# A new order for five engines: the masks of 14 attention tiles leave GpSimd, 38 unread products on TensorE

## The chip, the cores and the metric

The kernel runs on one core of a Trainium2 chip, as one launch. The metric is the device time in microseconds. The core has five engines that run side by side, each through its own list of instructions in order: TensorE (PE; its weight loads are shown as PEld), VectorE (DVE), ScalarE (ACT), GpSimd (POOL), and SyncE (SP), which here issues the transfers. They wait for each other by semaphores.

## The reference

The inputs are q, k, v of 8 batches, 8 heads, 576 positions and 64 columns, s of 8 x 8 x 576, and the weights of a gated unit. First comes a causal attention with a decay that a running sum of s gives, then a causal convolution of five taps, its sigmoid as a gate, and two 512 x 512 products:

```python
scores = scale * np.matmul(q, k.transpose(0, 1, 3, 2))
cum = np.cumsum(np.maximum(s, 0.0), axis=-1)
bias = -(cum[:, :, :, None] - cum[:, :, None, :])
scores = np.where(causal, -1000000000.0, scores + np.minimum(bias, 0.0))
attn = np.exp(scores - np.max(scores, axis=-1, keepdims=True))
attn = attn / (np.sum(attn, axis=-1, keepdims=True) + 1e-09)
x = np.matmul(attn, v)                 # heads side by side: (8, 576, 512)
for k in range(5):
    gate_pre += conv_w[k][None, None, :] * xp[:, k:k + S, :]   # xp: x with 4 zero rows ahead
gate = 1.0 / (1.0 + np.exp(-gate_pre))
out = gate * (x @ w_val) @ w_out
```

## The kernel before, in words

The work is cut into 32 tiles n = 4b + p: batch b, pair of heads p. ORDER is one long text of steps written as `name.index:engine:slots`, where S is SP, T TensorE, A ACT, V DVE and G POOL. Each engine gets its steps in the order of the text; how the steps of two engines stand to each other in the text does not matter. The slots name PSUM banks (0 to 7) or numbered buffers in SBUF. What is computed is the same for every order; the order, the choice of engine and the buffers decide who waits for whom.

The steps of one tile are these.

- `ld_q`, `ld_k`, `ld_t`, `ld_v`, `ld_s`, `ld_cw`, `ld_wv`, `ld_wo`: transfers into SBUF. V of a batch comes in five pieces (`ld_v.b.0` to `ld_v.b.4`, L471; for batch 0 by pairs of heads, L467 and L468), into one of two buffers `vst`.
- `c_q`, `c_k`, `cast_wv`, `cast_wo`: casts to bf16 (L373, a helper that copies on whatever engine it is given).
- `qt`, `qq`, `tt`: transposes of q and k on TensorE (L489, L629, L480), `qe` and `te` copy them out of PSUM (L373).
- `vp`: V times the decay weight `w`, for one pair of heads, on POOL (L474).
- `s0`, `s1`, `s2`: the scores of the tile in three steps (L505), each followed by an exponential `e0`, `e1`, `e2` on ACT into a buffer of P (L556). There are three buffers of P. `s4` and `e4` do the last 64 rows.
- The causal mask of the diagonal blocks is done in one of two ways. Where a step `mk.n` (or `ml.n`) stands in ORDER, POOL zeroes the upper part of P behind the exponential (L579). Where none stands, TensorE adds a large negative number in PSUM ahead of the exponential, with one further product for each of the two heads (`future`, L518).
- `av0`, `av`: P times V' (L594) into a pair of banks; `rec` and `nm` divide by the sums (L607, L613); `xt` transposes the result (L626), `xe` copies it to `xT` (L373).
- The convolution: `t1` on DVE (L665), then the taps `t2`, `t3`, `t4`. Each of these is either one step on DVE (L670), or a product `p2`, `p3`, `p4` on POOL (L654) or ACT (L652) and a sum on POOL (L673).
- `th`: the gate as a tanh on ACT (L690, L684); `val`: the product with `w_val` (L703); `glu`: gate times value on DVE (L712).
- `out` for each 128 rows of two batches (L723), `oe` copies the result out of PSUM (L373), `st` stores it (L731).
- `wu`: a product whose result nobody reads (L620).

Tiles 28 to 31, the last batch, are cut in two parts of 384 and 192 positions: scores `u0` to `u3`, exponentials `f0` to `f3` (L570), and `av.n.h`, `xt.n.h` and so on. At the end a check of the sums (`chk`, `cnt`, `cntc`, `flag`) decides whether a slow general path must run; with these inputs it does not.

In the list before, the P buffer of a tile was named by its score step, as the second slot of `s0.n` (`s0.0:T:0+1:0`), and kept for the whole tile.

Of the kernel before, what the change touches and what calls it, by code (L numbers as in the profile page):

```python
# [16 lines left out]
B, H, S, D = 8, 8, 576, 64  # L17
# [179 lines left out]
s2.0:T:6+7 wu.15:T:0 c_q.0.2:G e1.0:A qt.0.1.q:T:3 wu.16:T:0 qe.0.1.q:V wu.17:T:0 wu.18:T:0 e4.0.0:A wu.19:T:0  # L197
centre:V s0.1:T:4+5:1 ld_k.1.0:S:2 s2.1:T:2+3 e0.1:A qt.0.2.q:T:1 c_k.0.2:V decT:T:0 ld_cw:S e2.0:A qt.0.2.k:T:4
mk.1:G wu.20:T:5 ld_k.1.1:S qe.0.2.k:V wu.21:T:5 wu.22:T:5 qe.0.2.q:A s1.1:T:6+7 c_k.0.3:V e2.1:A s0.2:T:4+5:2
c_q.0.3:G ld_v.0.2:S expw:A qt.0.3.q:T:1 e1.1:A s4.0.1:T:2+3 qe.0.3.q:V vp.0.0:G qt.0.3.k:T:0 qe.0.3.k:V e4.0.1:A  # L200
ld_q.1.0:S:3 e0.2:A s2.2:T:6+7 s1.2:T:2+3 vp.0.1:G av0.0:T:0+1 e2.2:A av.0:T ld_v.0.3:S mk.2:G rec.0:V av0.1:T:4+5
e1.2:A nm.0:V av.1:T c_k.1.0:G:2 s0.3:T:6+7:0 rec.1:V s2.3:T:2+3 e0.3:A nm.1:V ld_t.1:S cwT:T:0 xt.0:T:1 c_k.1.1:G
cwc:V xt.1:T:4 e2.3:A wu.23:T:6 xe.0:V ld_q.1.1:S vp.0.2:G qq.1.1:T:0:7 t1.0:V:0 s4.0.2:T:2+3 s1.3:T:5+6 e4.0.2:A
xe.1:V c_q.1.0:A:0 s4.0.3:T:2+3 mk.3:G t3.0:V ld_v.1.2:S e4.0.3:A t1.1:V:1 e1.3:A ld_v.1.1:S av0.2:T:2+3 vp.0.3:G
av.2:T t2.0:V ld_v.1.0:S qe.1.3:A tt.1:T:5 ld_v.1.3:S qe.1.2:V p4.1:G:0 p4.0:A:1 ld_v.1.4:S ld_wv:S:4 av0.3:T:6+7
av.3:T te.1:A rec.2:V ld_t.2:S t4.1:G c_q.1.1:G nm.2:V s0.6:T:0+1:1 rec.3:V xt.2:T:5 nm.3:V e0.6:A t4.0:G s0.7:T:2+3:2
# [5 lines left out]
s1.7:T:6+7 nm.6:V e2.5:A xt.4:T:0 ld_v.2.2:S c_q.2:G:1 tt.2:T:1 xe.4:V th.0:A:2 av0.5:T:2+3 t1.4:V:2 av.5:T te.2:A  # L212
ld_v.2.4:S val.3.0:T:4 th.3:A:3 p4.4:G:1 rec.5:V val.3.1:T:1 nm.5:V e1.7:A val.1.0:T:5 glu.3.0:V t4.4:G xt.5:T:2
c_k.2:A:2 glu.3.1:V ld_v.2.1:S val.1.1:T:3 glu.1.0:V s2.7:T:6+7 glu.1.1:V qq.2.0:T:1:5 vp.1.3:G xe.5:V val.0.0:T:3
t2.4:V e2.7:A val.0.1:T:4 t1.5:V:1 p2.5:G:0 qe.2.0:A av0.7:T:6+7 glu.0.0:V glu.0.1:V ld_v.2.3:S val.2.0:T:3 t2.5:G
p3.5:A:1 t3.4:V av.7:T ld_v.2.0:S qe.2.1:A qq.2.1:T:4:2 ld_k.5:S:4 rec.7:V cast_wo:G nm.7:V val.2.1:T:0 qe.2.3:A
xt.6:T:5 glu.2.0:V xt.7:T:1 xe.6:V qe.2.2:A s0.9:T:6+7:1 glu.2.1:V s1.9:T:2+3 p4.5:G:0 xe.7:V out.0.2:T:0 e0.9:A
# [15 lines left out]
glu.8.1:V oe.0.5:A:5 ld_k.6:S:0 glu.10.1:V val.9.1:T:1 mk.14:G t4.11:V th.9:A:4 s2.14:T:2+3 qq.5.0:T:7:6 e2.14:A
glu.9.0:V c_k.5:G:0 av0.13:T:4+5 qe.5.0:V av.13:T qe.5.1:A val.11.0:T:0 ld_v.4.4:S rec.13:V glu.9.1:V th.11:A:1
s1.14:T:2+3 s0.15:T:6+7:0 nm.13:V vp.3.2:G e1.14:A val.11.1:T:1 glu.11.0:V xt.13:T:4 ld_v.4.0:S glu.11.1:V e0.15:A
mk.12:G s1.15:T:2+3 xe.13:V s2.15:T:0+1 st.0.5:S t1.13:V:2 e2.15:A qq.5.1:T:7:6 c_q.4:G:1 out.1.1:T:5 t2.13:V qe.5.2:A
qe.5.3:V av0.14:T:0+1 e1.15:A c_k.4:G:2 av.14:T out.1.2:T:7 rec.14:V p4.13:A:0 nm.14:V oe.1.1:A:2 qq.4.0:T:6:2
# [10 lines left out]
av0.18:T:1+2 ld_t.7:S e0.19:A av.18:T glu.15.1:V c_q.6:G:1 rec.18:V s1.19:T:6+7 glu.15.0:V s2.19:T:3+4 e1.19:A nm.18:V
out.1.4:T:0 t2.16:V e2.19:A xt.18:T:1 ld_v.6.0:S vp.5.3:G s0.20:T:6+7:1 xe.18:V tt.6:T:5 e0.20:A oe.1.4:V:1
qq.6.1:T:4:3 mk.19:G t1.18:V:2 th.16:A:1 st.1.3:S av0.17:T:6+7 te.6:V av.17:T qe.6.3:A c_q.7:G:2 ld_v.6.3:S  # L250
qq.6.0:T:0:2 rec.17:V qe.6.2:A nm.17:V out.1.6:T:5 t3.18:V qe.6.0:A ld_v.6.4:S av0.19:T:6+7 p2.18:G:1 oe.1.6:V:5
# [45 lines left out]
def main_path(ctx, tc, q, k, v, s, moe_w_val, moe_conv_w, moe_w_out, out, okcnt):  # L297
# [44 lines left out]
    Ps = kind("P", [128, 2, 1536], BF16)  # L342
# [315 lines left out]
    def tap(m):  # L658
# [181 lines left out]
```

## Time and profile before

| | before |
|---|---|
| median of 3 runs | 188.22 us |
| runs | 188.03, 190.68, 188.22 us |
| span of the profiled execution | 187.6 us |
| median less span | 0.6 us |
| mean granted clock of TensorE | 0.999 |
| instructions | 6637 |
| bytes read, written | 30.57 MB, 9.44 MB |

The page gives of the profiled execution its span alone, from the first to the last instruction; what lies around it is taken as the 0.6 us by which the median of the runs is longer.

The page lists for each engine its busy time and share of the span, then the span in 40 slices, the transfers by queue, the chain of work that ended last with each engine's share, and the costliest groups of instructions. A row of such a group ends with the busy time of all of them, the mean duration of one in ns, and, behind the second bar, the idle time of the engine just before them with what ended it. Busy times are unions: instructions of one engine that overlap are counted once, so a count times the mean is a little more than the busy time.

### The profile page before, as it was taken

To read this page: it belongs to the slowest core of one execution; us is meant where nothing else is said; L and a number is where in the kernel's file an instruction comes from. 1 tells how busy PE (TensorE), PEld (TensorE's weight loads), DVE (VectorE), ACT (ScalarE), POOL (GpSimd) and SP (SyncE) were. 2 spreads that over 40 slices of the span, in tenths; PEclk is the share of its full clock that TensorE was granted. 3 is DMA by queue.
4 is the path that set the end of the run, shared out by engine and by line. 5 is a ranking of instruction groups with operands and counts; after the bars stand their busy time and mean duration, and the time that the engine had idled before them with its cause. 6 is when DMAs were issued, how large, how long until landed. Compare 5 with 4: busy or idle time off the path is not lost.

```text
span 187.6 us, 6637 instructions
## 1 busy us (share of the span) xinstructions
PE 170.1 (91%) x2704; PEld 113.5 (60%) x2720; DVE 163.3 (87%) x321; ACT 170.6 (91%) x230; POOL 164.5 (88%) x149
## 2 busy tenths in 40 slices
PE   6898885888899998998978999999999999999991
PEld 2556573476757765576745667586566865776560
DVE  4355999878997899999999899998989899999980
ACT  2589899899999999999999999999999999999772
POOL 5267999899999999999978999999999989899610
PEclk9999999999999999999999999999999999999999
DMA  5998999999999999999298999899541003401164
GB/s 164 274 277 246 231 225 243 343 388 341 193 232 304 277 303 258 389 270 283 71 248 184 274 333 325 193 314 247 164 162 66 3 0 115 171 3 56 61 224 175
DMA packets 62283, 40.46 MB, mean 216 GB/s; under 512 B 47333, under 2 KB 49381, under 8 KB 62250
## 3 DMA queue, kind: packets, MB, share of 16 engines
q1 hardware_dynamic: 61706, 39.49, 77.1%
q8 instruction: 22, 0.36, 0.8%
q10 hardware_dynamic: 544, 0.52, 0.8%
q14 instruction: 11, 0.09, 0.2%
HBM read 30.57 MB, written 9.44 MB: 213 GB/s over the span
## 4 chain that ended last, share of the span: by engine, by line
PE 50%; ACT 15%; SPq 9%; DMA 8%; issue 6%; POOL 5%; DVE 4%; ACTq 0%; POOLq 0%; DVEq 0%
PE bank L723 14%; PE bank L703 11%; PE bank L594 10%; ACT P L556 9%; PE bank L505 7%; DMA vst<-in_v_dram 6%; SPq L435 3%; PE bank L629 3%; PE bank L626 3%; POOL gp L673 2%; DMA first<-in_k_dram 2%; ACT th L690 2%; SPq L471 2%; ACT QKT L373 2%; SPq L467 2%
## 5 line engine op out<-in xcount | busy, mean ns | idle before, releaser
L556 ACT ACTIVATE P<-bank 128x1024 bf16<-128x1024 f32 x84 | 82.9, 1042 | 4.1 <-PE bank L505 3.0
L670 DVE SCALAR_TENSOR_TENSOR gp<-bank,cwr,gp 128x574 f32<-128x574 bf16 (+6 forms) x72 | 52.3, 740 | 0.9 <-POOL gp L673 0.5
L673 POOL TENSOR_TENSOR gp<-gp,pr 128x572 f32<-128x572 f32 (+6 forms) x36 | 45.1, 1259 | 4.4 <-DVE gp L670 1.7
L474 POOL TENSOR_TENSOR Vp<-vst,w 128x650 bf16<-128x650 f32 x32 | 40.7, 1288 | 2.8 <-DMA vst<-in_v_dram 1.8
L505 PE MATMUL bank<-QKT 64*128 64x128 bf16 (+4 forms) x592 | 37.2, 237 | 4.8 <-ACT P L556 1.8
L703 PE MATMUL bank<-xT,wv 128*128 128x288 bf16 (+2 forms) x256 | 38.5, 287 | 1.1 <-ACT P L556 0.5
L594 PE MATMUL bank<-Vp,P 128*128 128x65 bf16 x960 | 36.0, 194 | 2.4 <-POOL Vp L474 1.1
L594 PEld LDWEIGHTS <-P 128*128 128x128 bf16 x960 | 33.2, 97 | 6.8 <-issue 1.5
L723 PE MATMUL bank<-wo,glu 128*128 128x512 bf16 x128 | 34.1, 380 | 1.5 <-issue 0.5
L505 PEld LDWEIGHTS <-QKT 64*128 64x128 bf16 x592 | 19.4, 94 | 22.3 <-issue 14.6
L712 DVE SCALAR_TENSOR_TENSOR glu<-th,bank 128x288 bf16<-128x288 f32 (+2 forms) x64 | 27.5, 445 | 2.0 <-ACT th L690 0.9
L703 PEld LDWEIGHTS <-wv 128*128 128x128 bf16 x256 | 22.4, 97 | 11.0 <-issue 4.8
L654 POOL TENSOR_TENSOR pr<-xT,cwr 128x572 f32<-128x572 bf16 (+6 forms) x28 | 28.3, 1020 | 0.6 <-ACT xT L373 0.6
L373 ACT COPY QKT<-bank 128x1024 bf16<-128x1024 bf16 (+1 forms) x26 | 24.2, 966 | 3.8 <-PE bank L489 2.9
L613 DVE TENSOR_TENSOR xn<-bank,recs 128x640 bf16<-128x640 f32 (+2 forms) x36 | 26.8, 745 | 0.6
L665 DVE SCALAR_TENSOR_TENSOR gp<-xT,cwr,bank 128x576 f32<-128x576 bf16 (+2 forms) x36 | 26.4, 741 | 0.7
L579 POOL TENSOR_SCALAR_AFFINE_SELECT P<-P 128x1024 bf16<-128x1024 bf16 (+1 forms) x22 | 22.3, 1021 | 4.2 <-ACT P L556 4.2
L690 ACT ACTIVATE th<-gp,cwr 128x576 f32<-128x576 f32 x28 | 22.0, 794 | 0.1
L723 PEld LDWEIGHTS <-glu 128*128 128x128 bf16 x144 | 12.4, 98 | 13.2 <-issue 1.6
L373 ACT COPY ot<-bank 128x512 f32<-128x512 f32 x26 | 15.2, 610 | 1.5 <-PE bank L723 1.0
L626 PE MATMUL bank<-ident,xn 128*128 128x128 bf16 x164 | 14.9, 219 | 0.7 <-ACT P L556 0.3
L373 POOL CAST qkb<-qkf 128x2048 bf16<-128x2048 f32 (+1 forms) x9 | 14.4, 1619 | 0.0
(66 smaller groups left out, 174.8 us busy)
## 6 DMA issues: line engine op xcount, KB each, us to landing
out_dram<-ot SPq DMA_DIRECT2D x36, 256.0 KB, 4.3
vst<-in_v_dram SPq DMA_DIRECT2D x28, 256.0 KB, 5.9
first<-in_q_dram SPq DMA_DIRECT2D x6, 512.0 KB, 6.0
first<-in_k_dram SPq DMA_DIRECT2D x6, 512.0 KB, 6.2
qkf<-in_q_dram SPq DMA_DIRECT2D x6, 512.0 KB, 6.7
qkf<-in_k_dram SPq DMA_DIRECT2D x6, 512.0 KB, 7.3
vst<-in_v_dram SPq DMA_DIRECT2D x15, 128.0 KB, 5.4
first<-in_q_dram SPq DMA_DIRECT2D x4, 256.0 KB, 5.3
```

Source lines behind the costliest of these rows:

```text
L373: (act.copy if e is act else e.tensor_copy)(dst, src)
L474: e.tensor_tensor(Vps[b % 2][:, :, HP[p]], vslot(b)[:, :, HP[p]], w[:, :, b * 8 + 2 * p:b * 8 + 2 * p + 2].unsqueeze(3).to_broadcast([128, ...
L505: pe.matmul(ps[:, hh, c0:c0 + nq], QKTs[b % 2][r, 1, p, k0:k0 + 128], QKTs[b % 2][r, 0, p, q0:q0 + nq], **kw)
L556: act.activation(out=Pt(n)[:, :, step * 512:(step + 1) * 512], in_=pair((f"s{step}", n)), func=AF.Exp, scale=0.125)
L594: pe.matmul(ps[:, o:o + 65], lhsT, Vps[b % 2][:, kb, 2 * p + w, :], start=(kb == 0), stop=(kb == qb))
L613: vec.tensor_tensor(xns[b % 2][:, g, p * 128:(p + 1) * 128].rearrange("t g (w d) -> t w g d", w=2), ps[:, :, :, 0:64], recs[:, n, :, g].un ...
L654: pool.tensor_tensor(pr, xTs[b % 2][:, c, 4 + lo - m:4 + hi - m], r.to_broadcast([128, hi - lo]), ALU.mult)
L670: vec.scalar_tensor_tensor(gp[:, lo:hi], xps(n, *h)[:, lo - m:hi - m], r, gp[:, lo:hi], ALU.mult, ALU.add)
L673: pool.tensor_tensor(gp[:, lo:hi], gp[:, lo:hi], prs[at[f"p{m}", n, *h][0]][:, lo:hi], ALU.add)
L703: pe.matmul(ps, wv[:, dc, c * 128:(c + 1) * 128], xTs[b % 2][:, dc, 4 + lo:4 + hi], start=(dc == 0), stop=(dc == 3))
L712: vec.scalar_tensor_tensor(glu2[:, c, o + lo:o + hi], th[:, lo:hi], 1.0, ps, ALU.add, ALU.mult)
L723: pe.matmul(bank_of(u, i), glu2[:, c, i * 128:i * 128 + 128], wo[:, c, :], start=(c == 0), stop=(c == 3))
```

## The change

ORDER is written anew. SP's 110 steps are the same in the same order, and ACT issues the same two first loads of k. On the other engines these things differ.

- Masks: `mk` stands for 5 tiles (11, 14, 19, 22, 23) instead of 18 (0 to 4, 6, 7, 9, 11 to 14, 18 to 20, 22, 24, 27), and `ml` for none instead of 4. All other tiles are masked by products on TensorE.
- Unread products: 38 instead of 32. Twelve stand ahead of the first transposes instead of eight.
- Choices of engine, by count of steps:

| steps | before | after |
|---|---|---|
| `qe` on ACT, DVE | 26, 10 | 27, 9 |
| `oe` on ACT, DVE | 26, 10 | 29, 7 |
| `xe` on ACT, DVE | 12, 24 | 9, 27 |
| `c_q`, `c_k` on ACT, DVE, POOL | 3, 4, 17 | 2, 2, 20 |
| `p2`, `p3`, `p4` on ACT, POOL | 8, 28 | 6, 31 |
| `t2`, `t3`, `t4` on DVE, POOL | 72, 36 | 71, 37 |

- The order of the steps on all engines but SP, the PSUM banks, and the buffers of P, `th`, `ot`, `pr`, `gp`, `qkb`. The slot of P now stands at the exponentials (`e0.0:A:0`), each of which names it.
- In the code, `Pt` looks the buffer up there, `split` is a set made ahead, and `val_part` loses a case that is not used.

The diff, cut: of ORDER the beginning, the stretch up to `av.4`, and the end.

```diff
 ORDER = """
-ld_k.0.0:A ld_q.0.0:S ld_k.0.1:A wu.0:T:0 ld_t.0:S wu.1:T:7 wu.2:T:0 wu.3:T:7 ld_s:S wu.4:T:0 ld_q.0.1:S wu.5:T:7
-wu.6:T:0 ld_q.0.2:S wu.7:T:7 c_k.0.0:V ld_k.0.2:S qt.0.0.k:T:0 wu.8:T:2 c_q.0.0:V ld_v.0.1:S qe.0.0.k:A qt.0.0.q:T:1
-wu.9:T:7 c_k.0.1:G qe.0.0.q:A wu.10:T:2 wu.11:T:7 s0.0:T:0+1:0 e0.0:A tt.0:T:2 ld_q.0.3:S relu:V qt.0.1.k:T:3
-wu.12:T:4 ld_k.0.3:S te.0:A wu.13:T:7 scan:V mk.0:G wu.14:T:0 ld_v.0.0:S qe.0.1.k:A s1.0:T:1+2 s4.0.0:T:4+5 c_q.0.1:A
...
-xe.2:V s2.6:T:6+7 e0.7:A qq.1.0:T:0:1 t1.2:V:2 mk.6:G p2.1:A:0 s1.6:T:2+3 t3.2:V qe.1.0:A ld_q.2:S:0 mk.7:G qe.1.1:V
-e2.6:A t3.1:V s1.4:T:0+1 e1.6:A s0.4:T:6+7:0 t2.2:V ld_k.2:S:1 xt.3:T:4 e0.4:A s0.5:T:2+3:0 t2.1:G t4.2:V s2.4:T:6+7
-xe.3:V wu.24:T:5 e2.4:A vp.1.0:G mk.4:G wu.25:T:5 t1.3:V:3 wu.26:T:5 wu.27:T:5 ld_wo:S:2 wu.28:T:5 e1.4:A s4.1.3:T:6+7
-ld_t.3:S t3.3:V wu.29:T:5 wu.30:T:5 e4.1.3:A s1.5:T:0+1 t4.3:V wu.31:T:5 th.2:A:0 ld_q.3:S:3 vp.1.2:G av0.4:T:6+7
-th.1:A:1 av.4:T t2.3:V e0.5:A vp.1.1:G cast_wv:G rec.4:V av0.6:T:4+5 nm.4:V av.6:T e1.5:A s2.5:T:2+3 rec.6:V
...
-u2.31:T:4+5:2 f3.30:A nm.28.1:V av.29.1:T:0 t1.31.0:V:1 ml.30:G val.28.0:T:1 f2.31:A t4.30.0:G rec.29.1:V t3.31.0:V
...
-st.3.1:S val.29.0:T:0 th.30.0:A:1 p4.28.1:G:0 t1.28.1:V:0 th.29.0:A:0 t2.31.0:V u3.31:T:5+6 t2.28.1:G out.3.3:T:1
-f3.31:A rec.30.1:V glu.29.0:V t4.28.1:G nm.30.1:V th.31.0:A:4 xt.29.1:T:7 ml.31:G val.31.0:T:0 glu.30.0:V xe.29.1:A
-t3.28.1:V xt.30.1:T:4 p3.29.1:G:1 av.31.1:T:3 glu.31.0:V xe.30.1:A th.28.1:A:2 out.3.0:T:2 t1.30.1:V:3 t1.29.1:V:2
...
+ld_q.0.0:S ld_k.0.0:A ld_k.0.1:A ld_t.0:S ld_s:S ld_q.0.1:S ld_q.0.2:S ld_k.0.2:S ld_v.0.1:S c_k.0.0:G c_q.0.0:A
+c_k.0.1:V wu.0:T:7 wu.1:T:6 wu.2:T:7 wu.3:T:6 wu.4:T:7 wu.5:T:6 wu.6:T:7 wu.7:T:6 wu.8:T:7 wu.9:T:6 wu.10:T:7
+wu.11:T:6 qt.0.0.q:T:0 qt.0.0.k:T:1 qe.0.0.q:A qt.0.1.k:T:2 qe.0.0.k:V ld_q.0.3:S qe.0.1.k:A wu.12:T:7 wu.13:T:6
+wu.14:T:7 s0.0:T:3+4 ld_k.0.3:S tt.0:T:5 e0.0:A:0 ld_v.0.0:S relu:V c_q.0.1:G scan:V te.0:A wu.15:T:2 wu.16:T:1
...
+wu.36:T:7 s4.1.3:T:6+7 s1.4:T:2+3 t3.3:V e4.1.3:A s0.4:T:4+5 e1.4:A:2 s1.5:T:6+7 ld_q.2:S:0 t4.3:V e1.5:A:1 s2.4:T:2+3
+t2.3:V ld_k.2:S:1 e2.4:A:2 t1.2:V:3 s2.5:T:6+7 vp.1.0:G t3.2:V e0.4:A:2 s0.5:T:2+3 ld_wo:S:2 t4.2:V vp.1.2:G e2.5:A:1
+wu.37:T:0 av0.4:T:4+5 av.4:T:4+5 t2.2:V ld_t.3:S e0.5:A:1 vp.1.1:G av.6:T:6+7 rec.4:V nm.4:V av0.6:T:6+7 th.3:A:1
+cast_wv:G th.2:A:2 rec.6:V av0.5:T:0+1 nm.6:V av.5:T:0+1 th.1:A:3 xt.4:T:2 rec.5:V s0.7:T:4+5 nm.5:V ld_q.3:S:3 xe.4:A
+s1.7:T:6+7 e0.7:A:2 val.0.1:T:3 t1.4:V:0 val.3.1:T:0 e1.7:A:2 c_q.2:G:1 t3.4:V val.1.1:T:1 val.3.0:T:4 glu.0.1:V
...
+av.28.1:T:1 f3.31:A:2 rec.29.1:V nm.29.1:V u2.31:T:4+5 t4.29.0:G rec.28.1:V th.31.0:A:0 xt.29.1:T:7 nm.28.1:V
+val.31.0:T:0 xe.29.1:V f2.31:A:2 t1.29.1:V:2 p2.29.1:G:0 xt.28.1:T:2 av.30.1:T:3 t4.29.1:V th.29.0:A:1 glu.31.0:V
+av.31.1:T:1 t2.29.1:G p3.29.1:A:1 xe.28.1:V out.3.0:T:4 t1.28.1:V:3 t3.29.1:G rec.31.1:V rec.30.1:V p4.28.1:G:0
...
 """
...
-    Pt = lambda n, h=None: Ps[at["s0" if h is None else f"u{2 * h}", n][1]]
+    split = lambda n: n in splits
+
+    def Pt(n, h=None):
+        steps = ("e0", "e1", "e2") if h is None else (f"f{2 * h}", f"f{2 * h + 1}")
+        return Ps[next(at[f, n] for f in steps if (f, n) in at)[0]]
...
     def val_part(n, hf):
-        two = at["val", n, 0][0]
-        j = two[hf] if isinstance(two, list) else at["val", n, hf][0]
+        j = at["val", n, hf][0]
...
+    splits = {int(name.split(".")[1]) for name, *_ in steps if name.startswith("u0.")}
```

More of the change, by code (lines that the diff above doesn't have):

```diff
@@ L198 @@
[L198 to L202, printed above, removed]
@@ L213 @@
[L213 to L217, printed above, removed]
@@ L233 @@
[L233 to L237, printed above, removed]
@@ L248 @@
[L248 to L251, printed above, removed]
-s2.20:T:3+4 xt.17:T:0 e2.20:A t4.18:V mk.20:G av.19:T ld_v.6.2:S out.1.5:T:5 xe.17:V qe.6.1:A rec.19:V t2.18:G
@@ new lines @@
+t3.11:V ld_v.4.2:S e0.13:A:0 val.10.1:T:1 ld_v.4.1:S t2.11:V vp.3.1:G val.9.0:T:2 e2.13:A:0 val.8.0:T:6 t4.11:V
+val.9.1:T:7 th.9:A:1 glu.10.1:V val.10.0:T:3 glu.8.0:V th.11:A:2 c_q.4:G:0 st.0.4:S val.11.0:T:4 glu.9.0:V glu.10.0:V
+s1.13:T:5+6 qq.5.0:T:1:2 glu.9.1:V e1.13:A:0 glu.11.0:V val.11.1:T:3 qe.5.0:V vp.3.0:G qe.5.1:A s2.14:T:4+5
+qq.4.0:T:7:6 glu.11.1:V e2.14:A:2 vp.3.3:G av.13:T:1+2 ld_k.6:S:0 glu.8.1:V qe.4.0:V av0.13:T:1+2 qe.4.1:A s1.15:T:4+5
+mk.14:G out.0.5:T:3 ld_v.4.4:S rec.13:V e1.15:A:0 nm.13:V c_k.4:G:1 s1.14:T:6+7 oe.0.5:A:0 ld_v.4.0:S xt.13:T:0
```

162 lines of the change are left out of this document (89 added, 73 removed).

## The prediction

> **What bounds the kernel now.** I read the page first: the busy shares, the clock, the shares of the chain that ended last. Then busy time by stage, then the chain and the waits at the two ends.
>
> ```profile
> span 187.6 us, 6637 instructions
> PE 170.1 (91%) x2704; PEld 113.5 (60%) x2720; DVE 163.3 (87%) x321; ACT 170.6 (91%) x230; POOL 164.5 (88%) x149
> PEclk9999999999999999999999999999999999999999
> PE 50%; ACT 15%; SPq 9%; DMA 8%; issue 6%; POOL 5%; DVE 4%; ACTq 0%; POOLq 0%; DVEq 0%
> 0.00:40.00 40.00, 32.59 (x502) 20.36 (x503) 29.31 (x57) 32.03 (x43) 30.68 (x37) 1.00 0.99 259
> 40.00:130.00 90.00, 84.87 (x1476) 58.70 (x1484) 83.44 (x150) 87.42 (x109) 88.10 (x67) 1.00 1.02 270
> 130.00:150.00 20.00, 19.41 (x332) 13.09 (x333) 18.74 (x34) 19.97 (x26) 19.61 (x17) 1.00 0.31 100
> 150.00:180.00 30.00, 29.74 (x383) 19.62 (x385) 29.49 (x73) 28.24 (x50) 26.10 (x31) 1.00 0.19 69
> 180.00:188.00 8.00, 3.49 (x22) 1.71 (x20) 2.31 (x11) 2.97 (x7) 0.00 (x0) 0.96 0.58 212
> ```
>
> The stage rows give, after the length, the busy time of PE, PEld, DVE, ACT, POOL, then clock, DMA share and GB/s. From 40 to 180 us ACT is busy 87.42 + 19.97 + 28.24 = 135.63 of 140: it idles 4.4 us in all. POOL is busy 88.10 of 90 between 40 and 130. No engine is loafing, so time can only go where load on ACT and POOL goes, and from the ends.
>
> TensorE looks as full (84.87 of 90), but its rows overlap:
>
> ```profile
> L518 PE MATMUL bank<-fut,fut 64*128 64x512 bf16 x20 | 3.8, 376 | 0.0
> 53.46 0.22 PE bank L518 x2
> 176.72 1.73 PE bank L723 x8
> 1.44 3.60 PE L620 MATMUL bank<-ident 128*128 128x512 bf16 x8 [1.44 <-POOL ident masks.py:199]
> ```
>
> Two mask products, each listed at 376 ns, took 0.22 us together on the chain; eight 512-column output products took 1.73 us, 0.216 each. So about half of a listed duration is pipeline, and PE has room that its 91% hides. I take 0.216 us for each pair of mask products (the two heads run side by side) and for each unread product once the array is fast. The Trainium skill says the same of this row: "Perfetto Trace Analysis", Identifying the Most-Contended Engine, calls matmul busy time a bad measure and points to weight-load busy, here 60%. By the listed durations the masks would cost 26 x 0.376 = 9.8 us, by the chain 2.8; the chain is measured, and the other reading is the slow rival below.
>
> **The front** is set by transfers:
>
> ```profile
> 28.08 5.99 DMA vst<-in_v_dram
> 34.23 1.28 POOL Vp L474
> 36.61 1.11 PE bank L594 x30
> 33.69 1.94 ACT L556 ACTIVATE P<-bank 128x1024 bf16<-128x1024 f32 x2 [0.54 <-PE bank L505]
> 37.77 2.85 ACT L556 ACTIVATE P<-bank 128x1024 bf16<-128x1024 f32 x3 [0.33 <-PE bank L594]
> PE bank L505 <- DVE QKT L373: 1.8, 1, 1.8
> PEld L594 <- POOL P L579: 0.7, 2, 0.5
> ```
>
> V of batch 1 lands at 34.1, is scaled (vp.1.0), and only then can av.4 run and free a buffer of P. SP's 110 steps stand in the same order in both lists, so this landing does not move by itself. ACT loses 0.54 and 0.33 us around this gate.
>
> **The change, part by part.** I counted the steps of both lists by engine; a half tile counts as 2/3 (384 columns) or 1/3 (192).
>
> ```profile
> L579 POOL TENSOR_SCALAR_AFFINE_SELECT P<-P 128x1024 bf16<-128x1024 bf16 x18 | 20.6, 1153 | 4.2 <-ACT P L556 4.2
> L579 POOL TENSOR_SCALAR_AFFINE_SELECT P<-P 128x256 bf16<-128x256 bf16 x4 | 1.7, 426 | 0.0
> L556 ACT ACTIVATE P<-bank 128x1024 bf16<-128x1024 f32 x84 | 82.9, 1042 | 4.1 <-PE bank L505 3.0 <-issue 0.4 <-PE bank L594 0.3
> L373 ACT COPY QKT<-bank 128x1024 bf16<-128x1024 bf16 x22 | 21.8, 1034 | 0.7 <-PE bank L629 0.6
> L373 ACT COPY ot<-bank 128x512 f32<-128x512 f32 x26 | 15.2, 610 | 1.5 <-PE bank L723 1.0 <-ACT ot L373 0.6
> L373 ACT COPY xT<-bank 128x576 bf16<-128x576 bf16 x7 | 4.6, 656 | 0.0
> L652 ACT ACTIVATE pr<-bank,cwr 128x572 f32<-128x572 bf16 x4 | 3.2, 789 | 0.0
> L373 ACT CAST qkb<-first 128x2048 bf16<-128x2048 f32 x1 | 1.9, 1898 | 0.0
> L373 ACT CAST qkb<-first 128x512 bf16<-128x512 f32 x1 | 0.6, 641 | 0.0
> L373 POOL CAST qkb<-first 128x512 bf16<-128x512 f32 x3 | 1.8, 610 | 2.2 <-DMA first<-in_k_dram 2.2
> L654 POOL TENSOR_TENSOR pr<-xT,cwr 128x572 f32<-128x572 bf16 x9 | 10.3, 1147 | 0.2 <-ACT xT L373 0.2
> L673 POOL TENSOR_TENSOR gp<-gp,pr 128x572 f32<-128x572 f32 x13 | 18.3, 1406 | 1.7 <-DVE gp L670 1.3
> L670 DVE SCALAR_TENSOR_TENSOR gp<-bank,cwr,gp 128x572 f32<-128x572 bf16 x15 | 12.0, 803 | 0.1
> L373 DVE COPY ot<-bank 128x512 f32<-128x512 f32 x10 | 6.8, 683 | 0.0
> L373 DVE COPY QKT<-bank 128x1024 bf16<-128x1024 bf16 x6 | 7.3, 1217 | 0.0
> ```
>
> *ACT.* QKT copies: four come from DVE, three go; net two whole less a half: 2 x 1.034 - 0.52 = +1.55. Output copies +3: 3 x 0.610 = +1.83. xT copies: net one whole less, -0.66. Casts: c_k.2 (1.898) and c_q.1.0 (half of it, 0.95) leave; net one of 512 columns comes, +0.64: -2.2. Tap products: 7.33 whole ones become 4.33: -3 x 0.789 = -2.37. Sum **-1.9 us**.
>
> *POOL.* Masks 18 to 5: -13 x 1.153 = -15.0; the four small ones, -1.7. Casts +1.9 + 0.95 + 0.61 = +3.5. Tap products +1.67 x 1.147 = +1.9; tap sums -1.33 x 1.406 = -1.9. Sum **-13.2 us**.
>
> *DVE.* -3 x 0.683, -2 x 1.217 + 0.6 for copies out, +0.45 for xT (a guess from its size, bounded by 0 and ACT's 0.66), two casts of about 0.6 less, taps +1.33 x 0.803: **-3.5 us**.
>
> *PE.* Masks by product: 13 x 0.216 = +2.8, the four small ones under 0.2 each. Six more unread products: +1.3. Fourteen masks leave POOL and one, 23, comes. Seven of the fourteen, n = 0 to 4, 6 and 7, lie in the front, where PE is busy 32.59 of 40 even by its long rows: ACT's work hides them. Without that cover they cost 0.22 each. The other seven lie where PE has room by the start-to-start times.
>
> *The first steps.* Twelve unread products instead of eight stand ahead of the first transposes. Here one takes 3.60 / 8 = 0.45, so the transposes start about 1.1 us later (12 x 0.43 from 1.44) and the first exponential about 0.5, since three casts now run side by side. The gate at 34 us hides it; uncovered it is 0.5 to 1.8. Queued behind these products is all of PE.
>
> *The gate.* Ahead of the exponential that waits for av.4's buffer (e0.7 in the new list, e0.5 in the old) ACT has 21 exponentials instead of 19, 2 x 1.042, and with its smaller steps about 2.9 us more by the listed durations. So the idle 0.54 + 0.33 = 0.9 should go: -0.9, between 0 and -2.9. What is late next is ACT itself.
>
> *The masks' path.* Exponential, mask on POOL, product becomes exponential, product. The waits for masks are small (the 0.7 above), but POOL holds 5% of the chain, 9.4 us; its load falls by 13.2 / 164.5 = 8%, so I take -0.7, between 0 and -4.4 (all of ACT's idle from 40 to 180).
>
> *The tail.*
>
> ```profile
> 173.94 0.27 PE bank L505 x4
> 176.00 0.17 PE bank L626 x3
> 176.17 0.55 PE bank L594 x18
> 183.47 0.59 ACT ot L373
> ```
>
> After the last score product PE works without pause to the last copy. There the new list has one more attention half (0.55) and one more group of transposes (0.17): **+0.7**, between 0 and +1.4. ACT's work behind its last exponential is as long as before.
>
> *Banks, buffers, stores.* Moved PSUM banks change no work; the wait they could add lies between -0.5 and +1.8 (the longest PE wait above). I take 0, nearest to the many waits under 0.5. Stores sit in SP's list ahead of later loads as before, so a late output copy could hold a load; the copies stand no later relative to their neighbours, so 0. The other edits rename tests (`split`, `Pt`) and emit nothing.
>
> Sum on the profiled execution: 187.6 - 1.9 - 0.9 - 0.7 + 0.7 = 184.8. The median of the runs, 188.22, is 0.6 above this span; so **185.4 us**.
>
> **The rivals.**
>
> *POOL set the pace.* For: 88.10 of 90. Against: few waits name it. Then the masks' path brings 2.2 to 4.4 instead of 0.7: 183.9 to 181.7, middle **182.8**.
>
> *Nothing comes of it.* ACT's 1.9 reappears as waits, since every tile still passes through all four engines, and 0.9 + 0.7 stay too: **188.2**. That is also where it ends if the new list doesn't do what it says, that is if ACT's busy time stays at 170.6. For: ACT holds only 15% of the chain. Against: its 4.4 us of idle.
>
> *TensorE becomes the bound* (slower). For: half the chain is PE. If the listed 376 ns were real, 26 of them are 9.8 us; half of that, PE's share of the chain, is 4.9: 187.6 + 4.9 + 0.6 = **193**. It decides once PE's true load fills a stage, which from 150 on (29.74 of 30, start-to-start in an unbroken row) is nearest. Against: of the masks only 24, 27 and the small ones lie there.
>
> *The clock falls.* At the start a product takes 0.45 instead of 0.216; a spell of 3.6 us like that one loses 1.8: **187.2**. Against: 1.00 in every stage, though PE once waited 1.8 us. The Trainium skill, "TensorE: Matmul & The Clock Gate", Part 1, has the array halve its rate after an idle window of about 3.4 us; no wait here is so long, and the trace's slow start agrees.
>
> **How the numbers follow.** Two per cent, 3.8 us, is about what a measurement of this kernel can tell from no change: faster is below 184.5, slower above 192.0. Forecast (184.5 to 187) 0.37; POOL 0.37; nothing 0.13; clock 0.03; TensorE 0.10. So faster 0.37, same 0.53, slower 0.10. The range leaves out the slow rival and a little below: 181.5 to 190.5. The forecast's own is 184.5 to 187.
>
> **What would show it.** Right: ACT's busy time near 168.7, POOL's near 151, DVE's near 160; the mask line on POOL 5 times, the mask products on PE (L518) 84 times instead of 50; vp.1.0 again near 34.2; ACT without idle at 37; clock 1.00. Wrong: vp.1.0 later than 35 (a transfer moved after all); waits of ACT for L505 above 5 us (masks slow the scores); ACT idle above 6 us from 40 to 180; a clock below 1.00.

## The result and the profile after

| | before | after |
|---|---|---|
| median of 20 runs each | 188.80 us | 189.88 us |
| ratio after / before, 95% interval | | 1.0057 [1.0038, 1.0076] |
| median span | 187.1 us (27 runs of the first set of experiments) | 188.0 us |
| median of time less span | 1.7 us (the same runs: 1.67 to 1.86) | 1.9 us |
| profiled execution: span, time | 187.6 us, not known | 187.3 us, 189.09 us |

In the experiments below, executions more than 1.5% above the fastest of their kernel are left out of ratios and medians.

The new order is 1.1 us slower where the forecast had it 2.8 us faster. ScalarE's load moved about as counted, GpSimd's by less. The first fence is the page of the new order: busy shares, clock, shares of the chain that ended last.

```profile
span 187.3 us, 6728 instructions
PE 174.0 (93%) x2742; PEld 114.7 (61%) x2760; DVE 165.2 (88%) x317; ACT 168.5 (90%) x228; POOL 154.4 (82%) x139
PEclk9999999999999999999999999999999999999999
PE 26%; DVE 25%; POOL 15%; ACT 9%; issue 9%; DMA 2%; SPq 0%; ACTq 0%; DVEq 0%; POOLq 0%
```

ACT is at 168.5 (168.7 was forecast), POOL at 154.4, 10 us below before (13 were forecast), and still the time doesn't follow. The chain of this execution has another make-up: TensorE held half of it, now it holds a quarter, and DVE and POOL hold 40%. The stages (length; busy PE, PEld, DVE, ACT, POOL; clock, DMA share, GB/s) tell where the room went:

```profile
0.00:40.00 40.00, 34.60 (x552) 21.38 (x552) 29.39 (x58) 31.87 (x43) 25.84 (x33) 1.00 0.99 266
40.00:130.00 90.00, 86.83 (x1464) 59.00 (x1473) 84.63 (x147) 87.46 (x112) 81.59 (x60) 1.00 1.03 274
130.00:150.00 20.00, 19.72 (x337) 13.65 (x338) 19.43 (x37) 20.00 (x27) 19.69 (x17) 1.00 0.18 67
150.00:180.00 30.00, 29.66 (x384) 19.16 (x386) 28.81 (x65) 26.55 (x46) 26.46 (x31) 1.00 0.20 72
180.00:188.00 8.00, 3.20 (x21) 1.47 (x18) 2.92 (x14) 2.60 (x6) 0.86 (x2) 0.94 0.54 201
```

POOL's relief lies wholly before 130 us (25.84 against 30.68, 81.59 against 88.10); from 130 on it has as much as before. ACT's relief is not in the full stage from 40 to 130 at all (87.46 against 87.42) but from 150 to 180 (26.55 against 28.24), where it waits. From 40 to 180 us ACT now idles 6.0 us instead of 4.4. The waits of the new order say on what (engine, line, what it waited for: us, times, longest):

```profile
POOL pr L659 <- ACT xT L375: 5.7, 3, 3.4
POOL pr L659 <- DVE xT L375: 5.5, 2, 3.4
ACT th L687 <- POOL gp L678: 1.9, 3, 0.9
```

POOL's list is in order: freed of the masks it stands before the next tap product and waits for a copy of `xT`, 11 us in five waits. In the tail ACT now waits for POOL's tap sums, a wait that before did not have. The end of the chain (start, us, what):

```profile
176.75 0.60 POOL gp L678
177.42 0.60 POOL gp L678
178.09 0.60 POOL gp L678
...
180.97 0.46 ACT th L687
181.46 0.36 DVE glu L714
181.87 1.27 PE bank L725 x5
183.21 0.59 ACT ot L375
```

Before, TensorE worked without pause up to the last copy; now, in this execution, TensorE's last products wait for gate and tap sums. How little that wait is worth, a_tail shows below.

### The profile page after: what moved, and what is told of

Read it like the earlier page. It is cut to its first block, busy times and chain, and to the rows that moved or that the text cites. A ratio compares the mean times of both kernels' runs of the same rounds, so it can differ in the third digit from the quotient of the medians.

```text
span 187.3 us, 6728 instructions
## 1 busy us (share of the span) xinstructions
PE 174.0 (93%) x2742; PEld 114.7 (61%) x2760; DVE 165.2 (88%) x317; ACT 168.5 (90%) x228; POOL 154.4 (82%) x139
## 4 chain that ended last, share of the span: by engine, by line
PE 26%; DVE 25%; POOL 15%; ACT 9%; issue 9%; DMA 2%; SPq 0%; ACTq 0%; DVEq 0%; POOLq 0%
DVE gp L675 8%; PE bank L705 6%; DVE gp L670 5%; PE bank L725 5%; POOL Vp L476 5%; PE bank L599 5%; PE bank L507 5%; POOL gp L678 5%; DVE xn L618 5%; ACT P L562 4%; POOL pr L659 4%; DVE glu L714 4%; DVE xT L375 2%; DMA out_dram<-ot 2%; ACT ot L375 2%
## 5 line engine op out<-in xcount | busy, mean ns | idle before, releaser
L675 DVE SCALAR_TENSOR_TENSOR gp<-bank,cwr,gp 128x573 f32<-128x573 bf16 (+5 forms) x71 | 54.5, 769 | 2.0
L678 POOL TENSOR_TENSOR gp<-gp,pr 128x572 f32<-128x572 f32 (+6 forms) x37 | 43.7, 1182 | 3.2 <-ACT pr L657 0.7
L659 POOL TENSOR_TENSOR pr<-xT,cwr 128x572 f32<-128x572 bf16 (+6 forms) x31 | 30.4, 987 | 11.8 <-ACT xT L375 5.7
L705 PE MATMUL bank<-xT,wv 128*128 128x288 bf16 (+2 forms) x256 | 36.9, 287 | 0.7 <-ACT P L562 0.7
L599 PEld LDWEIGHTS <-P 128*128 128x128 bf16 x960 | 32.1, 98 | 4.7 <-ACT P L562 1.2
L599 PE MATMUL bank<-Vp,P 128*128 128x65 bf16 x960 | 34.1, 194 | 0.7 <-ACT P L562 0.5
L714 DVE SCALAR_TENSOR_TENSOR glu<-th,bank 128x288 bf16<-128x288 f32 (+2 forms) x64 | 26.0, 448 | 1.6 <-ACT th L693 0.5
L375 ACT COPY QKT<-bank 128x1024 bf16<-128x1024 bf16 (+1 forms) x27 | 25.6, 990 | 1.9 <-PE bank L491 1.9
L375 POOL CAST qkb<-first 128x2048 bf16<-128x2048 f32 (+1 forms) x10 | 15.0, 1506 | 6.4 <-DMA first<-in_k_dram 3.3
L375 ACT COPY ot<-bank 128x512 f32<-128x512 f32 x29 | 17.2, 609 | 1.2 <-PE bank L725 1.2
(65 smaller groups left out, 168.5 us busy)
```

The costliest lines, as they stand in the source:

```text
L375: (act.copy if e is act else e.tensor_copy)(dst, src)
L599: pe.matmul(ps[:, o:o + 65], lhsT, Vps[b % 2][:, kb, 2 * p + w, :], start=(kb == 0), stop=(kb == qb))
L659: pool.tensor_tensor(pr, xTs[b % 2][:, c, 4 + lo - m:4 + hi - m], r.to_broadcast([128, hi - lo]), ALU.mult)
L675: vec.scalar_tensor_tensor(gp[:, lo:hi], xps(n, *h)[:, lo - m:hi - m], r, gp[:, lo:hi], ALU.mult, ALU.add)
L678: pool.tensor_tensor(gp[:, lo:hi], gp[:, lo:hi], prs[at[f"p{m}", n, *h][0]][:, lo:hi], ALU.add)
L705: pe.matmul(ps, wv[:, dc, c * 128:(c + 1) * 128], xTs[b % 2][:, dc, 4 + lo:4 + hi], start=(dc == 0), stop=(dc == 3))
```

## The experiments

All ratios are against the old order run beside them. "Span" is the median span of a kernel's runs. The new order stands at 1.0057.

**1. What lies around the span.** In the profiled execution of the new order 1.8 us lay outside the span, where the forecast had taken 0.6 for the old. Its trace shows a last fetch of 8192 bytes of instructions at 189.0 us, behind the span's end, which the old one's does not, and its VectorE program has 518 instructions, the old one's 512. So: the old order once more, the new one with 511, the old one with 520.

> The old order once more, so that each of its runs has a span beside its time. In the profiled executions the new order's time is 1.8 to 1.9 us longer than its span (189.09 against 187.3), the old one's 0.5 (188.03 against 187.6). Theory one (a step outside the span): every run here shows 0.4 to 0.6, and the median span is about 188.3, equal to or above the new order's 187.9. Rival (the 0.5 is the profiler's accident, the loss lies inside the span): the difference scatters, and is about 1.8 here too.

```diff
-        e.memset(vst[:, :, :, 64:65], 2.0)
+        pool.memset(vst[:, :, :, 64:65], 2.0)
... (and three more fills at the start)
```

> The new order with seven small fills at the start given to GpSimd, so that VectorE's program has 511 instructions instead of 518 (the old order's has 512); all that is computed stays. Theory one (the new order's time outside the span is VectorE's end that lies beyond the 512th instruction, for which 8192 more bytes are fetched at 189.0): time less span falls from 1.85 to 0.5, the span stays near 187.9, the median is 188.5, ratio 0.998 to the old order. Rival (the time outside has another cause): time less span stays 1.8, median 189.9, ratio 1.006.

```diff
     vec.memset(onec, 1.0)
+    spare = one.tile([128, 8], BF16, name="spare")
+    for j in range(8):
+        vec.memset(spare[:, j:j + 1], 0.0)
```

> The old order with eight fills of one column of a spare tile added at VectorE's start: 520 instructions instead of 512, about 0.5 us of work under the first transfers. Theory one (program length beyond 512): the span stays, time less span rises from 0.5 to 1.8, the median from 188.8 to 190.1, ratio 1.007. Rival (no step): ratio 1.000, time less span 0.5.

| | ratio, 95% | median | span | time less span |
|---|---|---|---|---|
| before_again | 1.0002 [0.9961, 1.0043] | 188.63 | 186.9 | 1.71 |
| a_dve_less | 1.0037 [1.0007, 1.0068] | 189.75 | 187.8 | 1.86 |
| b_dve_more | 0.9997 [0.9965, 1.0030] | 188.68 | 187.0 | 1.74 |

The program's length is worth nothing, and the theory falls. The late fetch does not follow that length either: a_dve_less, with 511 instructions, still has it (at 189.4), and b_dve_more, with 520, has none. The old order's own runs have 1.7 us outside the span. So the 0.6 of the forecast was no property of the kernel: it was the median of some runs less the span of another, longer execution, whose own time was probably near 187.6 + 1.7 = 189.3.

**2. The masks.** The 14 whole tiles and four small parts that changed sides, in four ways: by products in the old order; nowhere in the old order; nowhere in the new order; five of them back on POOL in the new order.

```diff
 b_masks_pe: mk.n of 14 tiles and ml.28 to ml.31 are taken out of ORDER
 b_no_masks, a_no_masks: besides, no product in their place
+    on_pool |= {("mk", n) for n in (0, 1, 2, 3, 4, 6, 7, 9, 12, 13, 18, 20, 24, 27)} | {("ml", n) for n in (28, 29, 30, 31)}
 a_masks_5: mk.9, mk.12, mk.13, mk.18, mk.20 on POOL, each behind its tile's last exponential
```

> The old order with nothing moved but the masks: the 14 of whole tiles that the new order also does by products, and the four small ones, leave GpSimd (POOL busy 164.5 to about 147, 32 more rows of the mask product on PE). Theory two, the forecast's (masks off GpSimd shorten the path exponential, mask, product): span 0.7 us shorter, ratio 0.996. Theory that POOL set the pace: 2 to 4 us shorter, 0.98. Rival (in-order queues: the time that leaves POOL becomes POOL's waits for the next copy, and nothing ahead of it comes earlier): ratio 0.998 to 1.002. Rival (TensorE pays): ratio above 1.010.

> The old order in which the same 14 tiles and four small parts get no mask at all, neither on GpSimd nor as a product (their diagonal blocks are left unmasked): GpSimd is relieved as in the run before, TensorE is not loaded. Theory now (TensorE's start-to-start load sets the pace from 40 us on, each mask product of two heads adds its 0.2 us, and GpSimd's relief is worth nothing): ratio 0.997 to 1.002, the steps at 40 to 180 us within 0.5 us of the old order's. Forecast's theory (the masks' path holds 0.7 us or more): ratio 0.996 or less. POOL as the pace: 0.98 to 0.988.

> The new order with no mask at all on the 14 tiles and four small parts that it masks by products and the old order masked on GpSimd (their diagonal blocks are left unmasked); no step moves. Theory now (TensorE's start-to-start load sets the pace, and these products are why the new order isn't 2 us shorter): 14 x 0.18 to 0.22 and 4 x 0.1 = 2.5 to 3.5 us less, median 186.3 to 187.4, ratio 0.985 to 0.993. Rival (the products hide in TensorE's pauses, the forecast's zero): 189.3 or more, ratio above 1.001.

> The new order with the masks of five tiles of the middle (9, 12, 13, 18, 20) given back to GpSimd, each right behind the tile's last exponential: five products of two heads fewer on TensorE, five selects of 1.15 us more on GpSimd, which has room (81.6 of 90 us busy from 40 to 130). Theory now (TensorE's load sets the pace): 5 x 0.2 to 0.28 = 1.0 to 1.4 us less, median 188.4 to 188.9 against the new order's 189.8, ratio to the old one 0.998 to 1.001. Rival (GpSimd's queue is in order, and the selects now hold the tap sums and V' behind them): 189.8 or more, ratio 1.006 or more.

| | ratio, 95% | median | span |
|---|---|---|---|
| b_masks_pe | 1.0081 [1.0042, 1.0121] | 190.74 | 189.0 |
| b_no_masks | 0.9973 [0.9942, 1.0005] | 188.69 | 186.9 |
| a_no_masks | 1.0041 [1.0008, 1.0074] | 189.70 | 187.8 |
| a_masks_5 | 1.0141 [1.0109, 1.0172] | 191.54 | 189.8 |

The rows of the mask products and of POOL's stage from 40 to 130 us in b_masks_pe:

```profile
L517 PE MATMUL bank<-fut,fut 64*128 64x512 bf16 x48 | 9.4, 382 | 0.0
40.00:130.00 90.00, 85.12 (x1484) 58.52 (x1489) 83.43 (x148) 87.15 (x108) 80.47 (x60) 1.00 0.99 270
```

POOL is relieved from 88.10 to 80.47 of 90 us and the kernel is slower. In the old order the products alone cost 1.0081 / 0.9973, that is 1.1% or 2.0 us (1.1 to 3.0 by the two intervals), of the 3.0 us that 14 pairs have at 0.216, and GpSimd's relief brings some 0.5 us (0.9973), by its interval between nothing and 1.1. Beside before_again the exponentials of b_masks_pe fall back in small steps, which fits products that find no pause: 0.7 us at tile 4, 1.1 at tile 14, 1.9 at tile 16, 2.5 at tile 25, 2.9 at the end. Not all of it is theirs: 0.4 is there at the first exponential, and b_no_masks has a like jump ahead of tile 16 (0.8 to 1.7). In the new order the same products cost nothing that shows: 0.16% between a_no_masks and the new order, with an interval of 0.4% either way. And to give five of them back to GpSimd costs 0.8% or 1.6 us, though GpSimd had 8 us free in that stage. My expectation that TensorE's load sets the pace of the new order fell here: what a mask costs differs from order to order. That the new order is laid around its products would explain it, but no run shows that. The six further unread products were in no run left out, so what they cost is not shown.

**3. One engine relieved, then all four, then the transfers.** The engines are relieved in the old order between 77 and 140 us (the masks all along), the transfers in both orders from about 36 us on:

```diff
 b_pe_less: one of four parts of 14 output products left out
+            if u == 1 or u == 2 and i < 5:
+                cs = range(3)
 b_act_less: six output copies on ScalarE, 64 columns instead of 512
+        n = 64 if (u, i) in ((1, 1), (1, 0), (1, 5), (1, 8), (1, 7), (2, 1)) else 512
 b_vec_less: a tap on VectorE of six tiles, 96 columns instead of 576
+            if m == 3 and n in (11, 12, 13, 14, 15, 16):
+                hi = lo + 96
 b_all_less: these three and b_no_masks together
 b_dma_less, a_dma_less: w_out loaded to a quarter, 18 stores of 128 columns instead of 512
+        n = 128 if u < 2 else 512
```

> The old order with one of four 512-row parts left out of 14 output products between 85 and 140 us (the outputs of these rows lack a part): 14 x 0.216 = 3.0 us less load on TensorE. Theory now (TensorE's pace): 2 to 3 us less, ratio 0.984 to 0.990. Rival (no single engine sets the pace): under 1 us less.

> The old order with six of ScalarE's output copies between 88 and 132 us cut from 512 to 64 columns (these rows of the output are partly not written afresh): 6 x about 0.45 = 2.7 us less load on ScalarE. Forecast's theory (each microsecond of ScalarE's load counts whole): 2 to 2.7 us less, ratio 0.986 to 0.990. Theory now (TensorE's pace): under 0.7 us less, ratio 0.996 to 1.001.

> The old order with one tap of six tiles between 77 and 106 us cut from 576 to 96 columns on VectorE (the gate of the other columns lacks that tap): 6 x about 0.5 = 3.0 us less load on VectorE. Theory now (TensorE's pace, with VectorE behind it): under 0.7 us less, ratio 0.996 to 1.001. Rival (VectorE's steps, 25% of the new order's chain and 4% to 14% of the old one's, set it): 2 us or more less, ratio under 0.990.

> The old order with the four reliefs at once that alone gave nothing: no masks of 14 tiles and the four small parts on GpSimd (17 us), 14 parts of output products (3.0 us of TensorE), six short output copies (2.7 us of ScalarE), six short taps (3.0 us of VectorE); all of these leave out or change part of the output. Theory of the joint pace (each engine alone is relieved in vain because another is as full): 2 to 3 us less, ratio 0.984 to 0.990. Theory of the gates (data lands when it lands): under 1 us less, ratio 0.995 to 1.001.

> The old order with the same transfers cut (w_out to a quarter, 18 stores to 128 of 512 columns; the output is not complete). Theory of the gates: the old order meets one at V of batch 1 (lands 33 to 34, used 0.16 later) and one at V of batch 4 (lands 97.75, used at 97.82), and its engines are 1 us behind the new order's at 60 to 90 us, so it gains less than the new order does: 0 to 1.5 us, ratio 0.992 to 1.000. Rival (transfers hide): 0.998 to 1.002.

> The new order with less to move and nothing else changed: w_out is loaded to a quarter (0.75 MB less) and the 18 stores of the first four batches write 128 of 512 columns (3.5 MB less), so the output is not complete. Theory of the gates (the transfer engines are busy 1.00 to 1.03 from the start to 130 us, the same list of transfers stands in both orders, and what the engines gain is lost again where data lands just in time: V of batch 2 at 55.9, used at 56.1; q of batch 4 at 78.2, used at 78.4): with 4.3 MB less these landings come 2 us or more earlier, and the time falls by 1.5 to 3 us, ratio to the old order 0.990 to 0.998 instead of 1.005. Rival (the engines set the pace, transfers hide): 1.003 or more.

| relieved | ratio, 95% | median | span |
|---|---|---|---|
| b_pe_less, TensorE by 3.0 us | 1.0004 [0.9967, 1.0041] | 189.28 | 187.6 |
| b_act_less, ScalarE by 2.0 us | 0.9987 [0.9955, 1.0020] | 188.57 | 186.9 |
| b_vec_less, VectorE by some 3 us | 1.0005 [0.9965, 1.0045] | 188.61 | 186.9 |
| b_no_masks, GpSimd by 16 us | 0.9973 [0.9942, 1.0005] | 188.69 | 186.9 |
| b_all_less, all four | 0.9976 [0.9946, 1.0007] | 188.49 | 186.8 |
| b_dma_less, 4.3 MB less | 0.9997 [0.9959, 1.0034] | 188.77 | 187.1 |
| a_dma_less, new order, 4.3 MB less | 1.0047 [1.0020, 1.0073] | 189.62 | 187.7 |

No relief shows, not even all four at once, whose interval ends at 1.0 us less; ScalarE's 2.0 us bring at most 0.9. Where ScalarE's 2 us went is in its waits from 85 to 135 us, first of before_again, then of b_act_less:

```profile
ACT QKT L373 <- PE bank L480: 0.4, 1, 0.4
ACT QKT L373 <- PE bank L629: 0.2, 1, 0.2
ACT P L556 <- PE bank L505: 0.2, 1, 0.2
```

```profile
ACT P L556 <- PE bank L505: 1.1, 4, 0.4
ACT QKT L373 <- PE bank L629: 0.6, 1, 0.6
ACT QKT L373 <- PE bank L480: 0.5, 1, 0.5
ACT P L556 <- PE bank L518: 0.3, 1, 0.3
```

0.8 us of waits became 2.5: most of what the copies gave up became waits for scores and transposes on TensorE, which did not come earlier. The transfers had been my theory for what holds both orders, since data landed just in time in the new one: q of batch 4 at 78.2, cast at 78.39. With 4.3 MB less (DMA share 0.90 instead of 1.03) that landing came at 73.5, and the cast stayed. GpSimd's rows around it, in the new order and in a_dma_less (the cast from `qkf` is meant):

```profile
78.39 1.89 POOL L375 CAST qkb<-qkf 128x2048 bf16<-128x2048 f32 x1
```

```profile
40.00:130.00 90.00, 87.64 (x1475) 59.06 (x1473) 84.62 (x148) 87.47 (x112) 80.96 (x60) 1.00 0.90 227
78.24 1.89 POOL L375 CAST qkb<-qkf 128x2048 bf16<-128x2048 f32 x1
```

So this landing just in time was no gate; the step was as late by its engine's own list. The transfers up to 34 us, V of batch 1 among them, were cut in no run: the gate of the front was not tested.

**4. The second half.** First the two orders joined at about 150 us, each one's body with the other's tail (slots renamed at the joint), then parts of the tail.

```diff
 nb_ot: new order up to rec.24, then what is left in the old one's order
 ob_nt: old order up to val.23.1, then what is left in the new one's order
```

> The new order up to about 150 us, and from there the old order's tail (buffer and bank numbers renamed so that they join). Theory (the new body arrives earlier, the new tail gives it back by tap sums on GpSimd and gate waits behind them): span 1 to 2.5 us under the new order's, median 187.5 to 188.8, ratio 0.992 to 0.999. Rival (the loss lies in the body, by TensorE's load): as the new order or later, ratio 1.005 to 1.012.

> The old order up to about 150 us, and from there the new order's tail. Theory (the new tail costs more): 1 to 2.5 us above the old order, ratio 1.005 to 1.013. Rival (the loss lies in the new body): the old order's time or less, ratio 0.995 to 1.001.

They gave 1.0354 [1.0320, 1.0389] and 1.0265 [1.0215, 1.0316]: both lose some 5 us or more at the joint, where the one's last steps are not in the place that the other's first steps expect. That tells nothing of either tail.

```diff
 a_tail
-p4.31.1:G:1 ... t4.31.1:G    and    -p3.30.1:G:0 ... t3.30.1:G
+t4.31.1:V                    and    +t3.30.1:V
 a_taps_less, b_taps_less (products and taps, on every engine)
+            if n >= 20:
+                hi = lo + 96
```

> The new order with the last two tap sums (of tiles 30 and 31, second part, 192 columns) as one step each on VectorE (0.42 us each) instead of a product and a sum on GpSimd (0.50 + 0.59 us each). Theory of the tail (GpSimd's chain of products and sums holds the last gate: its last sum ends at 180.94, the gate starts at 180.97, the value product waits): the last gate starts 0.5 to 1.1 us earlier, ratio to the old order 0.999 to 1.003 instead of 1.005. Rival (VectorE is as full there and its own queue takes the time): no change, 1.004 to 1.007.

> The new order with the taps two to four of tiles 20 to 31 done for 96 columns only, on whatever engine they stand (the gate of the other columns lacks them): from 125 us on GpSimd has some 25 us less to do and VectorE some 12. Theory now (the chain that ended last lies on GpSimd from 125 to 150 us and then on VectorE's and GpSimd's taps, and this is where the new order falls back by 1.7 us between 154 and 178): 1.5 to 3.5 us less, ratio to the old order 0.986 to 0.997. Rival (another engine, TensorE first, is as late): 1.002 or more.

> The old order with the same taps cut to 96 columns. Theory now (its tail is TensorE's, without a pause from 155 us, so the convolution is not on its path): 0 to 1 us less, ratio 0.995 to 1.001. Rival (the convolution's chain sets both tails): 1.5 us or more less, ratio under 0.992.

| | ratio, 95% | median | span |
|---|---|---|---|
| a_tail | 1.0064 [1.0038, 1.0091] | 189.68 | 187.8 |
| a_taps_less | 1.0009 [0.9986, 1.0033] | 188.91 | 187.0 |
| b_taps_less | 1.0030 [1.0002, 1.0059] | 189.39 | 187.7 |

To move the last two sums brings nothing. In the trace of a_tail TensorE works without pause from 176.7 us on, and the last copy starts at 183.11 instead of 183.21: what TensorE waited for the gate at the end was worth 0.1 us. To take the taps away from tile 20 on makes the new order 0.48% shorter than it was (0.2% to 0.8% by both intervals; 0.9 us), and with that it stands where the old order stands; the old order gains nothing from it. Less than the 1.5 us that I expected; that TensorE is nearly as late behind the taps would explain it, and the chain below fits that. This trace is of a long execution, though (187.5 us, the new order's was 187.3), so it shows who came last, not where the 0.9 us were won. a_taps_less, its chain's shares, the stage from 150 to 180, and the chain's end:

```profile
PE 57%; DVE 13%; ACT 11%; issue 5%; ACTq 0%; DVEq 0%
150.00:180.00 30.00, 29.66 (x399) 19.35 (x401) 24.94 (x67) 26.79 (x48) 10.42 (x29) 1.00 0.20 72
175.67 1.67 PE bank L729 x7
177.35 0.34 PE bank L631 x6
177.68 2.59 PE bank L729 x12
180.27 1.32 PE bank L709 x16
181.59 1.78 PE bank L729 x8
```

POOL has 10.42 of 30 us to do instead of 26.46, the POOL share of the chain (15%) is gone, and the tail is once more TensorE's without pause. So what the new order lost against the old one in its span, 0.9 us, is as large as what its taps on VectorE and GpSimd hold in its second half. That the two are equal is in part chance. Most executions of the old order hold a fall of TensorE's clock (see "The clock" below), fewer of the new one's do; where there is none, the median spans are 185.9 us for the old order, 187.85 for the new one and 186.85 for the new one with the short taps, so the taps are then about half of the loss. The other half was not found.

## Why the prediction was wrong, step by step

- **The sum's base**, "the median of the runs, 188.22, is 0.6 above this span": mis-sized. Measured 1.7 us in the old order and 1.9 in the new; the profiled execution of before lies 0.5 us above the median span. Term +0.6, measured +1.7.
- **ACT, -1.9**: the busy time fell as counted (170.6 to 168.5), the time of the kernel did not. The step that failed is "From 40 to 180 us ACT is busy ... so time can only go where load on ACT and POOL goes": a high busy share was read as a price for each microsecond. b_act_less took 2.0 us of ScalarE's work away and moved the time by -0.13% [-0.45, +0.20]: in the old order, and between 88 and 132 us, at most 0.9 of the 2.0 us are paid. Besides, the load that the change took away lay from 150 to 180, where ScalarE already idled 1.8 us; there no run relieved it.
- **The gate, -0.9**: half right. Around the gate at 34 us ScalarE now works on without idle, as forecast: six exponentials from 32.53 on, 5.60 us unbroken, while POOL takes up V' of batch 1 at 32.26.

```profile
32.53 5.60 ACT L562 ACTIVATE P<-bank 128x1024 bf16<-128x1024 f32 x6
32.26 3.76 POOL L476 TENSOR_TENSOR Vp<-vst,w 128x650 bf16<-128x650 f32 x3 [1.55 <-DMA vst<-in_v_dram]
```

  But av.4's sums were divided at 37.6 instead of 37.8: an idle that goes is not a step that comes earlier. vp.1.0 came at 32.26, not near 34.2; in two more runs with the old order's transfers V of batch 1 landed at 32.9 and 33.1, so much of this is the scatter of transfers.
- **The masks' path, -0.7**: not paid in time that shows. b_no_masks has -0.27% [-0.58, +0.05], 0.5 us, so in the old order a credit of 0.7 is neither shown nor excluded. The rival that GpSimd set the pace (182.8, by 2.2 to 4.4 us) is out by the same run; 88 of 90 us busy did not make it the bound.
- **Masks and unread products on TensorE at nothing**: right for the masks of the new order (a_no_masks), wrong as a rule, and untested for the unread products. The reading "PE has room that its 91% hides" holds only where a pause lies at the right place: in the old order some 2.0 of 3.0 us were paid. It is what the slow rival held, at 2 us instead of 4.9. The Trainium skill, "Perfetto Trace Analysis", Identifying the Most-Contended Engine, calls matmul busy time no good measure and offers weight-load busy instead. The trace agrees on the first (376 ns listed, 0.22 us for two on the chain); the weight-load share, 60%, did not tell the free room either.
- **The tail, +0.7**: the sign was right and the size near (0.9), the mechanism was not, so the size was luck. It was forecast as TensorE's extra half of `av` and transposes; what the runs show are the taps on VectorE and GpSimd from tile 20 on (a_taps_less), and in the trace ScalarE's three waits for them, 1.9 us.
- **First steps**: right. Twelve unread products took 5.06 us, the first exponential came at 8.4 instead of 7.9, and the front hid it.
- **DVE -3.5**: the sum of its instructions' durations fell by 2.8 us (181.2 to 178.4), the busy time rose from 163.3 to 165.2, since fewer of them overlap. POOL: 154.4 against about 151; here the sum of durations fell by 12.1 (170.3 to 158.2), near the 13.2 of the forecast, and the busy time by 10.1.
- **The clock**: 1.00 up to 180 us in both profiled executions (0.96 and 0.94 behind that, where the prediction has 1.00 in every stage), but not in most executions of the old order; the chance of 0.03 rested on one. In eight of the eleven traces of the old order and its variants TensorE's clock fell to 0.50 for 3.4 us, once or twice, between 24 and 37 us; in the seven of the new order and its variants it fell once, in a_masks_5. First before_again from 32 to 35 us and a pause of its TensorE ahead of that, then b_dve_more, which kept its clock (the last three figures of a stage are clock, DMA share, GB/s):

```profile
32.00:35.00 3.00, 3.00 (x17) 0.88 (x11) 2.89 (x5) 2.24 (x3) 2.68 (x3) 0.51 1.12 318
30.50 0.62 PE L505 MATMUL bank<-QKT 64*128 64x64 bf16 x12 [1.84 <-DVE QKT L373]
```

```profile
32.00:35.00 3.00, 2.70 (x30) 1.18 (x31) 2.89 (x5) 2.46 (x3) 3.00 (x3) 1.00 1.14 326
```

  From the exponential of tile 4 to that of tile 5 the old order takes 5.3 us in b_dve_more and 5.7 in the profiled execution of before, but 6.3 and 6.7 with a fall in between (before_again, b_taps_less). A fall takes 0.009 off the mean clock of 187 us, so the mean of a run tells whether it had one (0.991 or less, against 0.994 or more). Of 141 executions of the old order (before_again and the runs beside the experiments) 120 had one, with a median time of 188.9 us, and the other 21 a median of 187.75; of the new order's 20 executions 8 had one, with 190.0 against 189.7. So the new order is 1.1 us slower where both have the fall and 1.9 us slower where neither has, and the forecast's base, 187.6 us long at full clock, was an untypical execution (median span of the 21: 185.9). The forecast priced such a spell at 1.8 us; the medians differ by 1.2 in the old order and by 0.4 in the new. Whether the fall costs this, or late data makes both, is not shown. The Trainium skill, "TensorE: Matmul & The Clock Gate", Part 1, puts the half rate behind an idle window of about 3.4 us; here the longest pause of TensorE's products ahead of the fall was 1.84 us, so the measurement goes against that condition.

Without the three credits (-3.5) and with 1.7 for 0.6 the same sum gives 187.6 + 0.7 + 1.7 = 190.0, or 189.5 from the median span of 187.1; 189.88 was measured. That this comes so near is luck, since the 0.7 had another cause and the base was untypical. Of the rivals "nothing comes of it" was nearest, on a wrong base.

**What stays open.** That relief is not paid is shown for the old order from 77 to 140 us; which ring of waits holds its middle is not, since neither one engine, nor four, nor the transfers after 36 us moved it. No run was made to move the data that lands up to 34 us, or the clock there, though both differ between executions. Why the old order is 0.3% slower with fewer taps, its interval just above 1, was not followed up. No run that computes everything beat the old order.

## What to carry to other kernels

In a schedule where five in-order lists are laid tight around each other, a load taken away pays, as these runs suggest, only if what follows it on that engine is ready earlier too; before crediting it, look at who releases the next step, and give a credit of zero where that is another full engine. Load that is added is not symmetric: in one order it cost two thirds of its size (2.0 of 3.0 us, between 1.1 and 3.0 by the intervals), in the other nothing that shows. To join the halves of the two orders, or to move five masks back, lost more than was to be won (5 us or more, and 1.6). Look at the clock of many executions before one of them becomes the base. And take time and span from one execution: a median of runs less another run's span put 1.1 us into this forecast that no engine had anything to do with.

## What was not expected of the hardware

- Landing times of the same transfers scatter between executions by about 1 us (V of batch 1 at 34.07, 32.91 and 33.05 in kernels of the old order, 32.10 and 32.83 in kernels of the new one).
- The span of one and the same old order goes from 185.5 to 188.3 us (before_again), and much of that goes with a fall of TensorE's clock to half for 3.4 us in the front: a median of 187.1 us with it, 185.9 without.
- 4.3 MB fewer bytes, the DMA share from 1.03 to 0.90 between 40 and 130 us, changed the time by nothing measurable in either order: from 40 us on, transfer engines that are busy all the time did not set the pace.
- Eight more instructions on VectorE cost nothing that shows (0.9997 [0.9965, 1.0030]). The fetch of 8192 bytes of instructions behind the span's end goes with 1.9 instead of 1.7 us outside the span; what it costs was not tested.
